# A chunked recurrence and a gated two-product block on one core: both blocks' first products in a row, and weights narrowed in place

## The chip, the cores and the metric

One core of a Trainium2 chip runs the whole program. Its engines work side by side, each through its own queue in order: TensorE (PE in the profile; its weight loads are PEld) multiplies matrices into PSUM, VectorE (DVE), ScalarE (ACT) and GpSimd (POOL) work on elements, and SyncE (SP) issues most transfers. The metric is the device time of the program in microseconds.

## The reference

Two stages. For 4 sequences of 768 tokens and 8 heads of size 64, a state of 64 by 64 per head is decayed and updated at every token, and the query reads it:

```
for t in range(S):
    state = gamma * state + einsum('bhd,bhe->bhde', k[:, :, t], v[:, :, t])
    y[:, :, t] = scale * einsum('bhd,bhde->bhe', q[:, :, t], state)
x = y.transpose(0, 2, 1, 3).reshape(3072, 512)
h = x @ w_in                      # 512 x 2048
out = (h * sigmoid(1.702 * h)) @ w_out   # 2048 x 512
```

q, k and v are float32. The two weights come as 64-bit floats, which the kernel gets as pairs of 32-bit words, and which it has to turn into float32 itself.

## The kernel before

**Chunks and blocks.** The 3072 tokens are 24 chunks of 128, and a block is four chunks (512 tokens). A chunk takes three steps: `turn` (q and k transposed, for blocks 0 and 1 by TensorE, `pt`, for the others by VectorE; GpSimd scales k into `kd`), `attend` (`pa`, q times k for each head, masked by VectorE into `at`) and `finish` (`py`, the output, which VectorE scales into the block's input `X`; `pu`, the update of the state).

**Narrowing.** The weights arrive in 32 pieces of 512 KB, 16 of `w_in` (into tile `W1`) and 16 of `w_out` (into `W2`). `fetch` loads a piece into one of three raw buffers, and `narrow` turns its pairs of words into floats in seven steps, each over 128 partitions by 512 elements: ScalarE takes the high word's magnitude (line 171), GpSimd clamps it (172), VectorE shifts it, joins the sign and cuts out the exponent (173, 174, 175), ScalarE scales the low word (176), GpSimd multiplies it by the exponent (177), and VectorE adds both into the weight tile (180). The raw buffers and two sets of three scratch buffers lie in the part of `W2` that is filled later (slots 4 to 6). The last thing in `narrow` is the next `fetch`, which waits until the raw buffer is free.

**Two forms of a product.** A block's first product (`up`) and second (`down`) exist in a plain form (`up0`, `down0`: 16 steps f of four multiplications of 128 by 128 by 512) and in a form with seven sub-products in place of eight (`up`, `down`), which needs sums of the weights (`sums_w1`, `sums_w2`, on GpSimd), of X (`sums_x`) and of the hidden layer G (`sums_g`). Each step f of the plain first product reads pieces 2p and 2p+1 with p = f // 2, and each step f of the second reads piece 16 + f. Between the products, `hidden` applies the gate: a sigmoid on ScalarE into `sg`, and a multiplication by VectorE (line 253) out of the PSUM tile `ph`. `ph` and the second product's `po` share four PSUM buffers.

**Order of the work.** TensorE's order is the order in which the program is written. The other queues are ordered by the compiler's scheduler. Before, the program runs: the four chunks of block 0 with eight narrowings; block 0's first product, plain, with one narrowing per step; block 0's second product, plain, with the rest of the narrowings, the steps of block 1's four chunks between its steps, and `sums_w1`; then for block 1 and each later one `up` and `down` in the seven-product form, the next block's chunks lying between the units of `down`. `sums_w2` runs beside block 1's `up`.

## Time and profile before

| | us |
|---|---|
| median of 3 runs (lowest, highest) | 781.69 (781.29, 781.89) |
| profiled execution, its own time | 782.11 |
| its span | 780.3 |
| PE busy in the span | 725.1 (93%) |
| DVE busy | 368.6 (47%) |
| POOL busy | 206.3 (26%) |
| ACT busy | 153.4 (20%) |

The profile is of one execution; its time is 0.42 us above the median of the runs. Busy shares are means over stages of different kinds, so they are read stage by stage. A duration includes what an instruction waits after it has started, so the same operation can show two lengths. In the rows, `W` stands for W1 and W2 alike, and the raw and scratch buffers, which lie in W2, have that name too.

### The profile page before, as it was taken

What the parts mean: (1) busy time and instruction counts of PE and PEld (TensorE: products, weight loads), DVE (VectorE), ACT (ScalarE), POOL (GpSimd) and SP (SyncE); (2) the same over time, 40 slices, a digit from 0 to 9 for tenths busy, and PEclk for the clock granted to TensorE, in tenths of its full rate; (3) what the DMA queues carried; (4) which work ended last, traced back from release to release, by engine and by line L of the source; (5) the groups of instructions that cost most, each with busy time, mean ns of one, the idle gap of its engine ahead of it and who ended that gap; (6) DMA issues with size and microseconds to landing.
All of it is one profiled execution on the core that took longest, in us unless ns stands there. A gap on an engine that the chain in (4) does not pass through costs nothing.

```text
span 780.3 us, 9581 instructions
## 1 busy us (share of the span) xinstructions
PE 725.1 (93%) x3648; PEld 572.4 (73%) x3648; DVE 368.6 (47%) x547; ACT 153.4 (20%) x253; POOL 206.3 (26%) x195
## 2 busy tenths in 40 slices
PE   4679677499999999999999999999999999999998
PEld 3454222155568888888888888888888888888886
DVE  3678868761144336334436434445334364244251
ACT  3233334310103310013300023300033200033100
POOL 2776665584140004020014220012300022200030
PEclk9879878699999999999999999999999999999999
DMA  8634323312241003340022331022430030100001
GB/s 202 185 113 149 134 108 109 133 29 55 45 109 23 1 15 77 56 99 14 1 54 53 84 60 22 1 50 55 85 71 1 0 69 13 42 1 1 1 13 41
DMA packets 142253, 46.27 MB, mean 59 GB/s; under 512 B 129920, under 2 KB 135552, under 8 KB 142208
## 3 DMA queue, kind: packets, MB, share of 16 engines
q1 hardware_dynamic: 135504, 39.10, 21.5%
q10 hardware_dynamic: 6704, 6.57, 2.5%
q8 instruction: 29, 0.48, 0.2%
q14 instruction: 16, 0.13, 0.1%
HBM read 39.33 MB, written 6.29 MB: 58 GB/s over the span
## 4 chain that ended last, share of the span: by engine, by line
PE 77%; DVE 11%; POOL 7%; issue 3%; DMA 1%; SPq 0%; ACT 0%; POOLq 0%; DVEq 0%
PE pd L363 30%; PE px L312 18%; PE py L312 13%; PE po L272 5%; PE py L227 4%; POOL W L177 3%; PE pu L237 3%; PE pa L210 3%; DVE W L174 3%; DVE W L180 2%; DVE W L173 2%; PE py L223 2%; DVE W L175 1%; POOL W L172 1%; DMA W<-in_moe_w_in_dram 1%
## 5 line engine op out<-in xcount | busy, mean ns | idle before, releaser
L363 PE MATMUL pd<-W,G 128*128 128x256 f32 x1120 | 250.3, 381 | 0.4 <-DVE G L303 0.3
L363 PEld LDWEIGHTS pd<-W,G 128*128 128x128 f32 x1120 | 210.1, 190 | 30.8 <-DVE G L303 1.2
L312 PE MATMUL px<-X,W 128*128 128x256 f32 x640 | 148.7, 379 | 0.0
L312 PEld LDWEIGHTS px<-X,W 128*128 128x128 f32 x640 | 121.6, 190 | 17.0 <-issue 0.5
L312 PE MATMUL py<-X,W 128*128 128x256 f32 x480 | 113.4, 379 | 0.0
L312 PEld LDWEIGHTS py<-X,W 128*128 128x128 f32 x480 | 91.2, 190 | 12.4
L201 POOL TENSOR_TENSOR kd<-kn_in,cold 128x512 f32<-128x512 f32 x20 | 22.2, 1110 | 294.3 <-PE pu L237 200.4
L260 PE MATMUL ph<-X,W 128*128 128x512 f32 x128 | 65.8, 671 | 16.9 <-DVE G L253 16.9
L272 PE MATMUL po<-W,G 128*128 128x512 f32 x128 | 61.8, 628 | 10.4 <-DVE G L253 10.4
L213 DVE TENSOR_TENSOR at<-pa,mask 128x512 f32<-128x512 f32 x48 | 30.9, 685 | 83.6 <-PE pa L210 83.5
L260 PEld LDWEIGHTS ph<-X,W 128*128 128x128 f32 x128 | 26.6, 214 | 55.4 <-issue 30.9
L304 POOL TENSOR_TENSOR G<-G 128x512 f32<-128x512 f32 x20 | 29.0, 1449 | 111.5 <-DVE G L303 107.0
L272 PEld LDWEIGHTS po<-W,G 128*128 128x128 f32 x128 | 24.3, 199 | 39.2 <-issue 24.9
L252 ACT ACTIVATE sg<-G 128x512 f32<-128x512 f32 x60 | 37.8, 631 | 64.0 <-DVE G L322 38.3
L177 POOL TENSOR_TENSOR W<-W 128x512 f32<-128x512 f32 x32 | 43.5, 1360 | 25.8 <-DVE W L175 25.8
L253 DVE TENSOR_TENSOR G<-G,sg 128x512 f32<-128x512 f32 x60 | 41.3, 689 | 17.4 <-ACT sg L252 17.4
L227 PE MATMUL py<-at,v_in 128*64 128x128 f32 x384 | 32.2, 303 | 11.3 <-DVE at L213 11.3
L180 DVE TENSOR_TENSOR W<-W 128x512 f32<-128x512 f32 x32 | 30.3, 946 | 26.4 <-POOL W L177 26.1
L171 ACT ACTIVATE W<-W 128x512 f32<-128x512 f32 x32 | 21.6, 675 | 87.7 <-DVE W L180 79.1
L227 PEld LDWEIGHTS py<-at,v_in 128*64 128x64 f32 x384 | 24.5, 150 | 17.1 <-DVE at L213 13.7
L210 PEld LDWEIGHTS pa<-qT,kT 64*128 64x128 f32 x384 | 24.1, 193 | 15.4 <-issue 7.3
L322 DVE TENSOR_TENSOR G<-py,p 128x512 f32<-128x512 f32 x20 | 13.8, 692 | 44.4 <-PE py L312 44.4
(66 smaller groups left out, 620.5 us busy)
## 6 DMA issues: line engine op xcount, KB each, us to landing
W<-in_moe_w_in_dram SPq DMA_DIRECT2D x16, 512.0 KB, 4.0
W<-in_moe_w_out_dram SPq DMA_DIRECT2D x16, 512.0 KB, 3.2
v_in<-in_v_dram SPq DMA_DIRECT2D x24, 256.0 KB, 3.3
out_dram<-o ACTq DMA_DIRECT2D x24, 256.0 KB, 2.3
kn_in<-in_k_dram SPq DMA_DIRECT2D x21, 256.0 KB, 3.7
q_sq<-in_q_dram SPq DMA_DIRECT2D x256, 16.0 KB, 1.8
k_sq<-in_k_dram SPq DMA_DIRECT2D x256, 16.0 KB, 1.7
q_in<-in_q_dram SPq DMA_DIRECT2D x8, 256.0 KB, 5.2
```

The source lines that it names most:

```text
L177: pool.tensor_mul(r, r, e)
L180: dve.tensor_add(w, m.rearrange(shape, **sizes), r.rearrange(shape, **sizes))
L210: pe.matmul(p[:, i, hp, :], KT[j][r, hp, :], QT[j][r, hp, :], start=True, stop=True)
L213: dve.tensor_mul(AT[j][:, i], p[:, i], mask[:, i])
L227: pe.matmul(y[i * D:(i + 1) * D, hp, :], vn[:, 2 * hp + i, :], a[:, i, hp, :], start=(not c and hp == 0), stop=(hp == HP - 1), skip_group_ ...
L252: act.activation(s, h, AF.Sigmoid, scale=1.702)
L253: dve.tensor_mul(g, h, s)
L260: pe.matmul(h, w, X[:, c // 2:4:2, c % 2, :], start=(c == 0), stop=(c == 3))
L272: pe.matmul(PO[n], G[:, p, 2 * half + ab, t0:t0 + P], w, start=(f == 0), stop=(f == NFF - 1))
L304: pool.tensor_sub(g[1], g[1], g[0])
L312: pe.matmul(acc[:, u, :], W1[:, 2 * d + u, sa, c, :], X[:, sb, c, :], start=(start and u == 0 and c == 0), stop=(stop and c == 1), skip_gr ...
L363: pe.matmul(p0[:, n, :], G[:, p, sa, n * P:(n + 1) * P], W2[:, sb, p, :], start=(new and p == 0 and n == 0), stop=(last and p == NP - 1), ...
```

## The change

1. **Order.** Block 1's first product now runs in the plain form, right after block 0's first product and ahead of block 0's second. Block 1's chunks, which lay between the steps of block 0's second product, now lie between the steps of block 0's first. Block 1's second product stays in the seven-product form. So `sums_x` is not needed for block 1; `sums_w2` moves to block 0's second product and `sums_w1` to block 1's second. Within block 0, chunk j+1's `turn` is written ahead of chunk j's `finish`, and chunk 4's `turn` comes with block 0.
2. **Places.** Block 1's X lies in slot 6 of W2 (`X1`). Block 0's hidden layer, whose tile G now takes block 1's, lies in slots 4 to 6 of W1, slots 4 to 6 of X and a small tile (`g0`). Since these are not one run, the gate's multiplication of block 0 is two instructions of 256 elements. qT, kT, kd and at of the first eight chunks lie in G, in two sets.
3. **Narrowing in place.** There is no scratch: magnitude and exponent are made in the destination, sign and value in the raw buffer's high words, the scaled low word in its low words. These raw operands have a step of two words. There are four raw buffers. The clamp goes from GpSimd to VectorE.
4. **Loads.** The first eight chunks' q and k are loaded two chunks ahead in `turn`, v in `finish`; block 2's first loads (32 small ones for q and k of a chunk) are written into block 1's first product.

```diff
-    NRAW, NTMP = 3, 2
+    NRAW = 4
...
-            lo, hi = x[:, :, 0], x[:, :, 1]
-            m, e, r = TMPS[i % NTMP]
-            mu, eu = m.bitcast(U32), e.bitcast(U32)
+            (w, _, m), x = PIECES[i], RAWS[i % NRAW]
+            mu = m.bitcast(U32)
+            two_runs = x.rearrange("p (a b) two -> p a b two", a=2)
+            lo, hi = two_runs[:, :, :, 0], two_runs[:, :, :, 1]
 
             act.activation(m, hi.bitcast(F32), AF.Abs, scale=2.0 ** 16)
-            pool.tensor_scalar(m, m, F64_MOST * 2.0 ** 16, F64_LEAST * 2.0 ** 16, op0=ALU.min, op1=ALU.max)
+            dve.tensor_scalar(m, m, F64_MOST * 2.0 ** 16, F64_LEAST * 2.0 ** 16, op0=ALU.min, op1=ALU.max)
             dve.tensor_scalar(mu, mu, 3, None, op0=ALU.logical_shift_left)
-            dve.scalar_tensor_tensor(mu, hi, 0x80000000, mu, op0=ALU.bitwise_and, op1=ALU.bitwise_or)
-            dve.tensor_scalar(eu, mu, 0xFF800000, None, op0=ALU.bitwise_and)
+            dve.scalar_tensor_tensor(hi, hi, 0x80000000, mu, op0=ALU.bitwise_and, op1=ALU.bitwise_or)
+            dve.tensor_scalar(mu, hi, 0xFF800000, None, op0=ALU.bitwise_and)
+            r = lo.bitcast(F32)
             act.activation(r, lo, AF.Copy, scale=2.0 ** -52)
-            pool.tensor_mul(r, r, e)
+            pool.tensor_mul(r, r, m)
...
-        dve.tensor_mul(g, h, s)
+        for g, h, s in [(g, h, s)] if not isinstance(g, list) else [(g[i], h[:, i], s[:, i]) for i in range(2)]:
+            dve.tensor_mul(g, h, s)
...
+    turn(0)
     for j in range(CB):
-        if j + 2 <= CB:
-            load(j + 2)
-        turn(j)
         attend(j)
         narrow(1)
+        turn(j + 1)
         finish(j)
         narrow(1)
+    between = chunks(1)[1:]
     for f in range(NFF):
-        up0(f)
+        up0(0, f)
+        if f < NP or f % 4 == 3:
+            narrow(1)
+        if between and f >= 2:
+            between.pop(0)()
+    for f in range(NFF):
+        up0(1, f)
         narrow(1)
...
+        if f >= NFF - 2:
+            load(2 * CB + f - NFF + 2)
     for f in range(NFF):
         down0(f)
-        narrow(1)
-        if between and f >= 2:
-            between.pop(0)()
         if f % 4 == 3:
-            sums_w1(f // 2 - 1)
-    sums_x()
+            sums_w2(f // 2 - 1)
     for m in range(1, NB):
-        for d in range(NP // 2):
-            up(d)
-            if m == 1:
-                sums_w2(2 * d)
-            if m + 1 < NB and d < 2:
-                load((m + 1) * CB + d)
         between = chunks(m + 1) if m + 1 < NB else []
+        if m > 1:
+            for d in range(NP // 2):
+                up(d)
+                if m + 1 < NB and d < 2:
+                    load((m + 1) * CB + d)
         for n, unit in enumerate(down(m)):
             unit()
+            if m == 1 and n % 8 == 3:
+                sums_w1(n // 4)
```

**TensorE, from block 0's last chunk on, before** (`ph` is the first product, `po` block 0's second, `px` and the `py` of line 312 block 1's first, W_72 is W1 and W_73 is W2):

```order
L223 MATMUL py<-qT,state_81 128x128 x4
L227 MATMUL py<-at,v_in 64x128 x8
L237 MATMUL pu<-v_in,kd 128x128 x4
L260 MATMUL ph<-X,W_72 128x512 x64
L272 MATMUL po<-W_73,G 128x512 x12
L194 MATMUL pt<-ident,q_in 128x128 x4
L194 MATMUL pt<-ident,kn_in 128x128 x4
L272 MATMUL po<-W_73,G 128x512 x4
L210 MATMUL pa<-qT,kT 128x128 x8
```

The same engine now, from block 1's last chunk, between the steps of block 0's first product (`ph<-X`), to block 1's first (`ph<-W_73`, whose input X1 lies in W2) and block 0's second:

```order
L292 MATMUL ph<-X,W_72 128x512 x4
L245 MATMUL py<-G,state_82 128x128 x4
L249 MATMUL py<-G,v_in 64x128 x8
L262 MATMUL pu<-v_in,G 128x128 x4
L292 MATMUL ph<-X,W_72 128x512 x12
L292 MATMUL ph<-W_73,W_72 128x512 x64
L304 MATMUL po<-W_73,W_72 128x512 x6
L304 MATMUL po<-W_73,X 128x512 x2
```

Block 1's 64 multiplications of 512 columns stand ahead of block 0's second product, and nothing of a chunk stands between the steps of the second product any more.

**VectorE, in block 0's first product, before** (173, 174, 175 and 180 are narrowing, 253 is the gate):

```order
L173 TENSOR_SCALAR W_73<-W_73 128x512
L174 SCALAR_TENSOR_TENSOR W_73<-W_73 128x512
L175 TENSOR_SCALAR W_73<-W_73 128x512
L173 TENSOR_SCALAR W_73<-W_73 128x512
L253 TENSOR_TENSOR G<-ph,sg 128x2x256
L180 TENSOR_TENSOR W_72<-W_73 128x2x2x128
```

The same engine now, in block 0's first product (178 is the clamp, 179, 180, 181 and 188 or 191 the other steps of narrowing, 279 the gate, 253 and 267 the end of chunk 6):

```order
L181 TENSOR_SCALAR W_73<-W_73 128x2x256
L279 TENSOR_TENSOR W_72<-ph,sg 128x256
L279 TENSOR_TENSOR X<-ph,sg 128x256
L253 TENSOR_TENSOR W_73<-py,rowd 128x4x128
L267 COPY state_82<-pu 64x4x64 x2
L191 TENSOR_TENSOR W_73<-W_73 128x2x256
L180 SCALAR_TENSOR_TENSOR W_73<-W_73 128x512
L178 TENSOR_SCALAR W_73<-W_73 128x2x256
L181 TENSOR_SCALAR W_73<-W_73 128x2x256
L179 TENSOR_SCALAR W_73<-W_73 128x2x256
```

The clamp has joined VectorE's queue, the gate is two rows, and the chunks' rows lie among the narrowings. The last narrowing addition stands behind the gate of step 1 of block 1's first product:

```order
L279 TENSOR_TENSOR G<-ph,sg 128x2x256
L181 TENSOR_SCALAR W_73<-W_73 128x2x256
L179 TENSOR_SCALAR W_73<-W_73 128x2x256
L180 SCALAR_TENSOR_TENSOR W_73<-W_73 128x512
L191 TENSOR_TENSOR W_73<-W_73 128x2x256
L181 TENSOR_SCALAR W_73<-W_73 128x2x256
L279 TENSOR_TENSOR G<-ph,sg 128x2x256
L191 TENSOR_TENSOR W_73<-W_73 128x2x256
L279 TENSOR_TENSOR G<-ph,sg 128x2x256 x14
```

All but two of the gates of block 1's first product stand behind all narrowing.

More of the change, by code (lines that the diff above doesn't have):

```diff
@@ L111, in load @@
         if j < 2 * CB:
-            plain("q", q, "q_sq", 2)
-            plain("kn", k, "k_sq", 2)
+            if "q" in what:
+                plain("q", q, "q_sq", 2)
+                plain("kn", k, "k_sq", 2)
         else:
@@ L124, in load @@
                 plain("kn", k, "kn", 1)
-        plain("v", v, "v", 2)
+        if "v" in what:
+            plain("v", v, "v", 2)
     w1v = moe_w_in.bitcast(U32).rearrange("(c p) (f two) -> p c f two", p=P, two=2)
     w2v = moe_w_out.bitcast(U32).rearrange("(f p) (e two) -> p f e two", p=P, two=2)
-    stage = W2[:, 4:7].rearrange("p s n e -> p (s n e)")
-    NRAW, NTMP = 3, 2
-    RAWS = [stage[:, 1024 * i:1024 * (i + 1)].bitcast(U32).rearrange("p (n two) -> p n two", two=2)
-            for i in range(NRAW)]
-    TMPS = [[stage[:, 1024 * NRAW + 512 * (3 * i + t):1024 * NRAW + 512 * (3 * i + t + 1)] for t in range(3)]
-            for i in range(NTMP)]
+    NRAW = 4
+    RAWS = [W2[:, 4 + i // 2, i % 2 * 4:i % 2 * 4 + 4].rearrange("p n e -> p (n e)").bitcast(U32)
+            .rearrange("p (n two) -> p n two", two=2) for i in range(NRAW)]
     PIECES = []
@@ L404 @@
     load(1)
-    fetch()
-    fetch()
+    for _ in range(NRAW - 1):
+        fetch()
     make_identity(nc, ident)
@@ L418 @@
         dve.memset(t, 0.0)
-    for j in range(CB):
-        if j + 2 <= CB:
-            load(j + 2)
-        turn(j)
-        attend(j)
-        narrow(1)
-        finish(j)
-        narrow(1)
-    for f in range(NFF):
-        up0(f)
-        narrow(1)
-    narrow(1)
     def chunks(m):
```

67 lines of the change are left out of this document (48 added, 19 removed).

## The prediction

> **What bounds the kernel now.** I read first the windows of the trace, cut where the work changes: block 0's attention up to the first gate (62.7 us), the stage up to the last narrowing addition (171.2), block 0's second product and block 1's first (to 276.3), and the rest.
>
> ```profile
> core 0: us, PE busy (x) PEld busy (x) DVE busy (x) ACT busy (x) POOL busy (x), PEclk, DMA share, GB/s
> 10.00:62.70 52.70, 37.46 (x225) 28.24 (x226) 35.16 (x55) 16.94 (x29) 32.84 (x33) 0.87 0.58 158
> 62.70:171.20 108.50, 81.25 (x175) 33.29 (x174) 81.84 (x110) 36.99 (x63) 72.08 (x65) 0.84 0.34 114
> 171.20:276.30 105.10, 104.41 (x501) 74.09 (x500) 36.83 (x56) 19.86 (x34) 24.36 (x22) 1.00 0.21 43
> 276.30:780.30 504.00, 499.81 (x2744) 435.30 (x2742) 212.60 (x319) 77.96 (x128) 74.15 (x68) 1.00 0.18 38
> ```
>
> From 171.2 on TensorE is busy 104.41 of 105.10 us and then 499.81 of 504.00: nothing but its own work counts there. Before that no engine is full. In the second row VectorE has 81.84 and GpSimd 72.08 of 108.50, so I looked at how these two stand to each other, in the instructions in order of time, VectorE's first and then GpSimd's in the same stretch.
>
> ```profile
> 109.41 1.09 DVE L180 TENSOR_TENSOR W<-W 128x512 f32<-128x512 f32 x1 [0.85 <-POOL W L177]
> 110.42 0.41 DVE L173 TENSOR_SCALAR W<-W 128x512 uint32<-128x512 uint32 x1
> 110.87 0.69 DVE L174 SCALAR_TENSOR_TENSOR W<-W 128x512 uint32<-128x512 uint32 x1
> 111.59 0.72 DVE L175 TENSOR_SCALAR W<-W 128x512 uint32<-128x512 uint32 x1
> 112.23 0.41 DVE L173 TENSOR_SCALAR W<-W 128x512 uint32<-128x512 uint32 x1
> 112.68 1.63 DVE L174 SCALAR_TENSOR_TENSOR W<-W 128x512 uint32<-128x512 uint32 x1
> 114.24 0.68 DVE L253 TENSOR_TENSOR G<-ph,sg 128x512 f32<-128x512 f32 x1
> 114.84 0.68 DVE L180 TENSOR_TENSOR W<-W 128x512 f32<-128x512 f32 x1
> ```
>
> ```profile
> 108.11 1.27 POOL L177 TENSOR_TENSOR W<-W 128x512 f32<-128x512 f32 x1 [1.21 <-DVE W L175]
> 109.34 0.61 POOL L172 TENSOR_SCALAR W<-W 128x512 f32<-128x512 f32 x1
> 111.29 0.75 POOL L172 TENSOR_SCALAR W<-W 128x512 f32<-128x512 f32 x1 [1.33 <-ACT W L171]
> 112.40 1.37 POOL L177 TENSOR_TENSOR W<-W 128x512 f32<-128x512 f32 x1 [0.36 <-DVE W L175]
> ```
>
> Line 174 takes 0.69 us at 110.87, but 1.63 at 112.68, where GpSimd's multiplication had begun at 112.40: that ends at 113.77, and 174 ends 0.54 later. Line 180 at 109.41 is stretched to 1.09 by the clamp of 109.34. So VectorE's narrowing steps, which read and write SBUF, and GpSimd's operations take turns: their lengths alone add up. The gate (253), which reads PSUM, is not stretched; the groups of the stage below show it at a mean of 680 ns, and likewise the chunks' steps 213, 230 and 246. [...]
>
> ```profile
> L253 DVE TENSOR_TENSOR G<-ph,sg 128x512 f32<-128x512 f32 x16 | 10.9, 680 | 0.2 <-ACT sg L252 0.2
> L213 DVE TENSOR_TENSOR at<-pa,mask 128x512 f32<-128x512 f32 x8 | 5.1, 686 | 0.1
> L230 DVE TENSOR_TENSOR X<-py,rowd 128x512 f32<-128x512 f32 x4 | 2.8, 689 | 4.2 <-PE py L227 4.2
> L246 DVE TENSOR_TENSOR state<-state,pu 64x256 f32<-64x256 f32 x6 | 2.5, 419 | 2.4 <-PE pu L237 2.3
> ...
> L177 POOL TENSOR_TENSOR W<-W 128x512 f32<-128x512 f32 x32 | 43.5, 1360 | 25.8 <-DVE W L175 25.8
> ...
> L244 POOL TENSOR_TENSOR state<-state,cold 64x256 f32<-64x256 f32 x8 | 6.2, 778 | 0.3
> L284 POOL TENSOR_TENSOR W<-W 128x512 f32<-128x512 f32 x4 | 6.0, 1493 | 0.0
> ...
> L201 POOL TENSOR_TENSOR kd<-kn_in,cold 128x512 f32<-128x512 f32 x4 | 4.2, 1044 | 7.9 <-issue 4.3 <-PE pu L237 3.6
> ...
> L289 POOL TENSOR_TENSOR W<-W 128x512 f32<-128x512 f32 x1 | 1.3, 1258 | 0.0
> ```
>
> **The sum of before, 10 to 171.2 us,** in lengths alone. VectorE: 32 pieces of 0.41 + 0.69 + 0.41 + 0.69 = 70.4; 16 gates of 0.68, 10.9; four chunks with 8 masks (5.5), 4 outputs (2.8) and 8 state steps of 0.42 (3.4): 93.0. GpSimd: 32 clamps of 0.61, 19.5; 32 multiplications of 1.27, 40.6; 22 weight sums (lines 281 to 290) of 1.26, 27.7; kd 4.2; state 6.2: 98.2. Together 191.2, in 161.2 us: 0.843 of the sum, 30 us being saved where PSUM-fed VectorE work runs beside GpSimd and where ends and starts overlap. The narrowing stage is that sum, and TensorE waits for it.
>
> **The change, part by part.** *Narrowing.* The clamp leaves GpSimd (0.61) and costs VectorE what the shift costs, 0.41, the nearest row. Multiplication, joins and addition stay; per piece 2.61 us of VectorE and 1.27 of GpSimd. The steps on raw words have a step of two now. Line 174 already reads such words and takes the 0.69 of line 180, whose operands are in a row: lower bound no cost, which I take. The upper bound is half speed for the stepped multiplication, 1.27 more per piece, and 0.69 for the exponent cut, 0.28 more.
>
> *Weight sums.* All 16 sums of W1 leave the stage, and 4 sums of W2 (5.0) are left in it. The others come behind the last narrowing, under 55 us of block 0's second product and then block 1's second; 28 of them are 35 us of GpSimd. W1's sums are needed only at block 2. Without that cover, 35 us.
>
> *Gates and chunks.* Block 0's gates become 32 of 256 elements, at the 0.42 of line 246's size 13.4; two whole ones of block 1 come in front of the last addition (1.4). Eight chunks instead of four lie in the stage: 16 masks 11.0, 8 outputs 5.5, 14 state steps 5.9; on GpSimd 8 kd 8.3 and 12 state steps of 0.78, 9.4. Two transpositions for block 2 at an output's 0.69, 1.4.
>
> Sum: VectorE 32 x 2.61 + 13.4 + 1.4 + 11.0 + 5.5 + 5.9 + 1.4 = 122.1; GpSimd 40.6 + 8.3 + 9.4 + 5.0 = 63.3; together 185.4. At the same 0.843, 156.3 us: the last addition begins at **166.3**, 4.9 us earlier. The factor's bounds: the 14.7 us by which PSUM-fed work grows (22.6 to 37.2) may all lie under GpSimd, 12.4 earlier; or the 30 us saved shrink with GpSimd's share to 19.3, 9.8 later.
>
> *TensorE behind it.* The chain that ended last has TensorE's lengths when it doesn't wait.
>
> ```profile
> 171.18 1.74 DVE W L180
> ...
> 208.94 0.87 PE pt L194 x8
> ...
> 213.25 1.09 PE pa L210 x16
> ...
> 217.97 0.89 PE py L223 x8
> 218.87 1.02 PE py L227 x16
> 219.89 1.09 PE pu L237 x8
> 220.98 6.87 PE po L272 x16
> 227.85 1.73 PE px L312 x8
> ...
> 276.19 6.91 PE pd L363 x32
> ```
>
> Two plain steps are 6.87 us, 3.44 each; a seven-product first product is 276.19 - 227.85 = 48.3. Block 1's, in plain form, is 16 x 3.44 = 55.0, so TensorE has 6.7 us **more** to do. But it does it earlier. Before, 105.0 us lie between the last addition (171.18) and block 1's second product (276.19). Now, four PSUM buffers let TensorE be through step 4 when step 1's gate frees the next one, just ahead of the last addition: 11 steps are left (37.8), then block 0's second product (55.0), 92.8 us. Block 1's second product begins at 166.3 + 92.8 = 259.1, **17.1 us** earlier. Behind it the program is as it was, with 35 us of weight sums spread under it. The profiled execution's 782.11 becomes 765.0; the median is 0.42 lower, 764.6.
>
> *Chunk order and loads.* `turn` ahead of `finish` gives TensorE something to do while VectorE masks; I count nothing for it, since the sum above, not TensorE, sets the stage. Block 2's loads now lie in SP's queue between the fetches of `w_out`. Sixteen small ones took:
>
> ```profile
> 228.09 10.88 SPq L120 DMA_DIRECT2D q_sq<-in_q_dram  x16
> ```
>
> that is 0.68 us each, up to six between two fetches, 4.1 us. A fetch is let go when the piece four earlier is added, so it has three pieces of 156.3 / 32 = 4.9 us, 14.7, in hand: covered. Without that, up to 32 x 0.68 = 22 us.
>
> **The rivals.**
> 1. *TensorE sets the pace.* If narrowing hides better, the floor is TensorE's own work. Up to the first gate the sum falls from 61.5 (narrowing 18.7, chunks 11.7, GpSimd 31.1) to 54.9 (21.6, 11.7, 21.6), so at the first stage's 52.7 / 61.5 that gate comes at about 57. Then 16 steps (55.0) with chunk 4's rest, 5, 6 and 7 (17.0 from the chain's rows) are 72 us at full clock or 86 at the granted 0.84, and 32 steps more 110.0: block 1's second product then begins at 239 to 253, a gain of 23 to 37. For it: the PSUM-fed work. Against: the order puts most gates right behind an addition, when GpSimd has just finished. Time 755 (745 to 759).
> 2. *Serial coupling.* VectorE's queue now holds rows that wait for TensorE (chunks, gates) among the narrowings, and half the 30 us saved are lost: 170.4 in place of 156.3, a gain of 3, about 779. For it: each wait on TensorE holds the narrowing behind it. Against: TensorE has slack in that stage. If nothing at all were saved, 794.
> 3. *Stepped operands are slow* (the other side). The place is GpSimd's multiplication, which reads and writes every second word, and the exponent cut on VectorE, which reads so. It decides from 17.1 / (32 x 0.843) = 0.63 us per piece on. [...] For it: no row shows GpSimd on such operands. Against: line 174. [...]
> 4. *No change in effect*: the plain form's 6.7 us and the longer VectorE queue just cancel the earlier start; it is the end of rival 2 and has no chance of its own.
>
> **How the numbers follow.** Forecast 0.52 (765, its own range 752 to 774 from the factor's bounds), rival 1 0.18, rival 2 0.16, rival 3 0.14. A difference of 0.2% (1.6 us) is about what can be told from no change here. Faster: the first two and two thirds of rival 2, 0.80; within 0.2%: 0.05; slower: rival 3 and the end of rival 2, 0.15. The range takes in rival 1 and the cheaper part of rival 3: 749 to 787.
>
> **What would show it.** The last narrowing addition near 166 us, and TensorE without gaps from there; 92.8 us later the first `pd`. Line 184 at 1.27 us alone and line 181 at 0.41 say that stepped operands cost nothing. Both engines together still fill the stage, with GpSimd's share down by a third. Wrong would be: TensorE waiting in block 0's second product, additions later than 185 us, fetches that arrive after VectorE asks, or a first product in which TensorE never waits.

## The result, and the profile after

The changed kernel takes **759.47 us** (median of 4 runs, 757.97 to 760.20) against 781.79 for the kernel before on the same chip: a ratio of **0.9712** with a 95% interval of 0.9695 to 0.9729. The forecast was 765.0 us, with a range of 749 to 787.

The profiled execution's page gives TensorE this share of a span of 757.6 us (before: 780.3). Below it the windows of the trace after, cut where the work changes: up to 52.0 block 0's chunks, up to 161.6 the stage that ends with the last narrowing addition, up to 253.5 the rest of block 1's first product and block 0's second, then block 1's second product and all that follows.

```profile
PE 722.7 (95%) x3552; PEld 553.2 (73%) x3552; DVE 358.5 (47%) x579; ACT 145.2 (19%) x241; POOL 179.0 (24%) x159
```

```profile
core 0: us, PE busy (x) PEld busy (x) DVE busy (x) ACT busy (x) POOL busy (x), PEclk, DMA share, GB/s
10.00:52.00 42.00, 30.57 (x221) 24.55 (x222) 33.25 (x55) 17.25 (x29) 18.11 (x17) 0.88 0.79 191
52.00:161.60 109.60, 98.56 (x369) 51.48 (x368) 97.57 (x179) 42.07 (x72) 48.73 (x39) 0.94 0.53 141
161.60:253.50 91.90, 91.45 (x214) 40.32 (x213) 12.52 (x17) 7.17 (x12) 33.56 (x27) 1.00 0.05 10
253.50:757.60 504.10, 499.95 (x2745) 435.42 (x2743) 212.98 (x319) 77.44 (x127) 75.73 (x70) 1.00 0.19 39
```

The last window is what it was (504.10 against 504.00 us). The whole gain lies ahead of it: block 1's second product begins at 253.4 in place of 276.0. In the second window TensorE is now busy 98.56 of 109.60, VectorE 97.57 where the corresponding stage before had 81.84 of 108.50, and GpSimd 48.73 where it had 72.08. In the third window TensorE is busy 91.45 of 91.90.

The chain that ended last (start and length in us), from the last narrowing addition (191) over the gate (279) to block 1's second product:

```profile
161.61 1.74 DVE W L191
163.35 0.61 DVE G L279
...
164.00 34.60 PE ph L292 x80
198.60 54.93 PE po L304 x128
253.54 6.91 PE pd L395 x32
```

From 164.0 on TensorE has 80 matmuls of block 1's first product left, ten steps, then 128 of block 0's second. That is the shape the prediction gave it, with one step less.

What TensorE waited for between 44 and 175 us, before and after (total us, times, longest):

```profile
PE ph L260 <- DVE G L253: 16.9, 8, 4.3
PE po L272 <- DVE G L253: 10.4, 3, 5.2
PE py L227 <- DVE at L213: 3.6, 4, 2.7
```

```profile
PE py L249 <- DVE G L235: 9.5, 8, 3.1
PE ph L292 <- DVE G L279: 2.5, 3, 1.2
PE ph L292 <- DVE X L253: 1.7, 1, 1.7
```

Before, it waited for gates (253). Now it waits for the masks of block 1's chunks (235), and less. So two things are candidates for what sets the time of the changed kernel, and the experiments are built to tell them apart:

- **Theory A, the prediction's:** the lengths of VectorE's narrowing steps and of GpSimd's work add up, their sum sets when the last addition comes, and a fixed rest of TensorE work follows.
- **Theory B, its first rival's:** TensorE's own path sets the time: when its first `ph` starts, its own work, and what it waits for on the way. The narrowings matter only as far as masks and gates stand behind them in VectorE's queue.

TensorE's path can be balanced from its records: from the first `ph` to the first `pd` lies TensorE's own work, its waits, and half of the time in which it worked while its granted clock was half (before, eight `ph` that began at 81.93 took 5.40 us with 3.4 us at a granted 0.50 among them, and the eight at 88.89, at 1.00, 3.70). Before: 55.6 to 276.0 us, with 27.9 us of waits and 34.1 us at half clock, of which 10.2 lie inside waits and 23.9 are work. After: 50.1 to 253.4, with 11.5 us of waits and 13.7 at half clock, 0.7 inside a wait and 13.0 work. The 22.6 us are thus an earlier start (5.5), fewer waits (16.4) and less work at half clock (10.9 / 2 = 5.5), less 4.8 of added work (220.4 - 27.9 - 12.0 = 180.5 before, 203.3 - 11.5 - 6.5 = 185.3 after). The plain form adds 6.7; 0.9 goes because chunk 4's `turn` now lies ahead of the first `ph` (0.87 us in the chain before); 1.0 isn't traced.

### The profile page after: what moved, and what is told of

Its sections match the earlier page's. It is cut to its first block, busy times and chain, and to the rows that moved or that the text cites. A ratio compares the mean times of both kernels' runs of the same rounds, so it can differ in the third digit from the quotient of the medians.

```text
span 757.6 us, 9340 instructions
## 1 busy us (share of the span) xinstructions
PE 722.7 (95%) x3552; PEld 553.2 (73%) x3552; DVE 358.5 (47%) x579; ACT 145.2 (19%) x241; POOL 179.0 (24%) x159
## 4 chain that ended last, share of the span: by engine, by line
PE 76%; DVE 3%; POOL 1%; DMA 0%; issue 0%; ACT 0%; DVEq 0%; POOLq 0%; ACTq 0%
PE pd L395 31%; PE px L344 15%; PE py L344 11%; PE po L304 7%; PE ph L292 5%; PE pa L232 2%; PE py L249 2%; PE pu L262 2%; PE py L245 2%; DVE G L334 1%; DVE G L335 0%; DMA W<-in_moe_w_out_dram 0%; DVE W L180 0%; POOL W L184 0%; DVE G L333 0%; DVE W L191 0%
## 5 line engine op out<-in xcount | busy, mean ns | idle before, releaser
L344 PE MATMUL px<-X,W 128*128 128x256 f32 x512 | 119.0, 379 | 0.0
L344 PEld LDWEIGHTS px<-X,W 128*128 128x128 f32 x512 | 97.3, 190 | 13.2
L344 PE MATMUL py<-X,W 128*128 128x256 f32 x384 | 90.7, 379 | 0.0
L344 PEld LDWEIGHTS py<-X,W 128*128 128x128 f32 x384 | 73.0, 190 | 9.9
L292 PE MATMUL ph<-W,W 128*128 128x512 f32 x128 | 55.9, 595 | 2.5 <-DVE G L279 2.5
L292 PEld LDWEIGHTS ph<-W,W 128*128 128x128 f32 x128 | 24.1, 190 | 34.2 <-issue 28.9
L304 PE MATMUL po<-W,W 128*128 128x512 f32 x96 | 42.5, 592 | 0.0
L277 ACT ACTIVATE sg<-G 128x512 f32<-128x512 f32 x48 | 30.3, 631 | 50.9 <-DVE G L354 30.6
L279 DVE TENSOR_TENSOR G<-G,sg 128x512 f32<-128x512 f32 x48 | 33.1, 689 | 13.7 <-ACT sg L277 13.7
L277 ACT ACTIVATE sg<-ph 128x512 f32<-128x512 f32 x32 | 18.9, 594 | 60.6 <-PE ph L292 42.7
L184 POOL TENSOR_TENSOR W<-W 128x512 f32<-128x512 f32 x16 | 23.2, 1452 | 29.0 <-DVE W L181 15.7
L184 POOL TENSOR_TENSOR W<-W,W 128x512 f32<-128x512 f32 x16 | 22.0, 1375 | 30.7 <-DVE W L181 13.7
## 6 DMA issues: line engine op xcount, KB each, us to landing
W<-in_moe_w_in_dram SPq DMA_DIRECT2D x16, 512.0 KB, 3.8
W<-in_moe_w_out_dram SPq DMA_DIRECT2D x16, 512.0 KB, 3.4
```

Of the source, the lines that this page charges most:

```text
L184: pool.tensor_mul(r, r, m)
L277: act.activation(s, h, AF.Sigmoid, scale=1.702)
L279: dve.tensor_mul(g, h, s)
L292: pe.matmul(h, w, x[:, c // 2:4:2, c % 2, :], start=(c == 0), stop=(c == 3))
L304: pe.matmul(PO[n], g0(p, 2 * half + ab)[:, t0:t0 + P], w, start=(f == 0), stop=(f == NFF - 1))
L344: pe.matmul(acc[:, u, :], W1[:, 2 * d + u, sa, c, :], X[:, sb, c, :], start=(start and u == 0 and c == 0), stop=(stop and c == 1), skip_gr ...
```

## The experiments

For each kernel of this study, read from its trace: first `ph`, the last narrowing addition, the end of TensorE's last wait ahead of `pd` with the `ph` matmuls that TensorE then still had to do, its waits from the first `ph` on, and the first `pd`. The ratio is to the kernel before. Times of the trace are those of one execution, the last column is the median of several; for order_only and pool_order the traced execution was 2.3 and 2.5 us below that median. The recorded expectations call theory A the turn-taking theory; theory B appears there as rival 1 and as the lockstep theory.

| kernel | first `ph` | last addition | last wait ends, `ph` left | waits | first `pd` | median us, ratio (95%) |
|---|---|---|---|---|---|---|
| before | 55.6 | 171.2 | - | 27.9 | 276.0 | 781.8 |
| the change | 50.1 | 161.6 | 164.0, 80 | 11.5 | 253.4 | 759.47, 0.9712 (0.9695 to 0.9729) |
| inplace_old_order | 58.2 | 167.3 | - | 28.1 | 273.6 | 780.31, 0.9981 (0.9972 to 0.9990) |
| order_only | 47.1 | 164.9 | 167.3, 88 | 21.1 | 261.8 | 770.18, 0.9855 (0.9840 to 0.9870) |
| clamp_pool | 50.9 | 161.0 | 163.5, 104 | 18.5 | 263.2 | 769.11, 0.9839 (0.9823 to 0.9854) |
| no_clamp | 47.6 | 147.3 | 148.8, 104 | 12.6 | 250.2 | 756.07, 0.9669 (0.9653 to 0.9685) |
| turn_undone | 57.4 | 164.7 | 166.0, 96 | 12.6 | 262.3 | 768.84, 0.9838 (0.9824 to 0.9851) |
| sp_order | 51.1 | 164.5 | 165.8, 88 | 17.3 | 260.3 | 766.35, 0.9803 (0.9785 to 0.9821) |
| pool_order | 49.3 | 163.3 | 165.7, 72 | 13.1 | 251.6 | 760.14, 0.9716 (0.9696 to 0.9735) |
| mask_gap | 51.9 | 164.2 | 161.8, 88 | 14.3 | 255.0 | 759.80, 0.9721 (0.9707 to 0.9736) |
| paced | 49.1 | 189.2 | 68.5, 224 | 3.2 | 237.1 | 751.35, 0.9609 (0.9594 to 0.9624) |
| mul_vector | 45.6 | 149.5 | none | 0.0 | 229.6 | 735.97, 0.9408 (0.9394 to 0.9421) |
| mul_both | 46.4 | 168.6 | 170.4, 48 | 9.1 | 246.0 | 751.99, 0.9621 (0.9607 to 0.9634) |
| add_only | 34.6 | 89.0 | none | 0.0 | 217.4 | 723.93, 0.9263 (0.9251 to 0.9276) |

An edit changes more than the lines shown, because the compiler's scheduler orders VectorE's queue anew for each kernel. If clamp and multiplication are left aside, VectorE's order departs from that of the changed kernel within the first 23 of some 230 instructions (up to 260 us) in clamp_pool, no_clamp, turn_undone and mul_vector, at the 52nd in pool_order, the 87th in mask_gap and the 120th in sp_order. Differences between these kernels therefore hold the edit and a new order together, and no run here takes the two apart. mul_vector and mul_both have one and the same order on VectorE.

### The two halves of the change apart

**Narrowing in place, in the old order of blocks.** Into the kernel before went the new narrowing alone (four raw buffers, clamp on VectorE).

```
 # the kernel before, with
-            pool.tensor_scalar(m, m, F64_MOST * 2.0 ** 16, F64_LEAST * 2.0 ** 16, op0=ALU.min, op1=ALU.max)
+            dve.tensor_scalar(m, m, F64_MOST * 2.0 ** 16, F64_LEAST * 2.0 ** 16, op0=ALU.min, op1=ALU.max)
...
-            dve.scalar_tensor_tensor(mu, hi, 0x80000000, mu, op0=ALU.bitwise_and, op1=ALU.bitwise_or)
+            dve.scalar_tensor_tensor(hi, hi, 0x80000000, mu, op0=ALU.bitwise_and, op1=ALU.bitwise_or)
...
-            pool.tensor_mul(r, r, e)
+            pool.tensor_mul(r, r, m)
```

> The kernel before with the new narrowing alone (in place, four raw buffers, clamp on VectorE), its order of the work kept. By the prediction's sum: VectorE 32 x 2.61 + 10.9 + 11.7 = 106.1, GpSimd 98.2 - 19.5 = 78.7, together 184.8 in place of 191.2, the last addition 5.4 us earlier, about 776.4. If stepped operands or the longer VectorE queue eat that: 782 or more. If the changed kernel's whole gain lies in the narrowing: 760.

It gives 780.31 us: 0.2% faster, where the sum expected 776.4. The last addition comes 3.9 us earlier (5.4 by the sum), but the first `ph` starts 2.6 us later and TensorE's waits stay (28.1).

**The order of blocks, with the old narrowing.** Into the changed kernel went the old narrowing (three raw buffers, scratch for the three temporaries, clamp on GpSimd); block 1's input has a place of its own.

```
-    X1 = W2[:, 6].rearrange("p (s c) t -> p s c t", s=4)
+    X1 = const.tile([P, 4, 2, TH], F32, name="X1")
...
-    NRAW = 4
...
+    NRAW, NTMP = 3, 2
...
-            dve.tensor_scalar(m, m, F64_MOST * 2.0 ** 16, F64_LEAST * 2.0 ** 16, op0=ALU.min, op1=ALU.max)
+            pool.tensor_scalar(m, m, F64_MOST * 2.0 ** 16, F64_LEAST * 2.0 ** 16, op0=ALU.min, op1=ALU.max)
...
-            pool.tensor_mul(r, r, m)
+            pool.tensor_mul(r, r, e)
```

> The new order and places with the old narrowing (scratch buffers in slots 4 to 6 of W2, three raw buffers, clamp on GpSimd); block 1's X, and later qT, kT and at, in a tile of their own. By the turn-taking sum alone: 6.4 us more of GpSimd and VectorE than the change, about 765. Lockstep theory (TensorE, whose chunks wait for masks in VectorE's queue, sets the pace together with it): no better than the clamp on GpSimd alone, 769 or more, and with two scratch sets in place of four raw buffers rather 770 to 776. If the gain needs the narrowing in place: 780.

770.18 us, within what the lockstep theory expected; the sum alone gave 765. The order alone gives 11.3 us (0.0145 x 782), the narrowing alone 1.5 (0.0019 x 782), both together 22.3: the halves need each other. With the old narrowing TensorE waits 21.1 us in the new order, with the new one 11.5.

### Does the last addition set the end?

**The clamp back on GpSimd**, and **no clamp at all** (weights beyond its range are then not held).

```
-            dve.tensor_scalar(m, m, F64_MOST * 2.0 ** 16, F64_LEAST * 2.0 ** 16, op0=ALU.min, op1=ALU.max)
+            pool.tensor_scalar(m, m, F64_MOST * 2.0 ** 16, F64_LEAST * 2.0 ** 16, op0=ALU.min, op1=ALU.max)
```

> The changed kernel with the clamp back on GpSimd, all else as changed. Turn-taking theory (VectorE's SBUF steps and GpSimd's operations add up; the changed kernel's stage of 151.6 us is 0.818 of its sum of 185.4): the sum grows by 32 x (0.61 - 0.41) = 6.4 us, the stage by 5.2, about 764.7 us. Rival 1 (TensorE sets the pace of the stage): 759.5, no change. Rival V (VectorE's own queue sets it, GpSimd runs freely beside): VectorE loses 32 x 0.41 = 13.1 us, about 749.

```
-            dve.tensor_scalar(m, m, F64_MOST * 2.0 ** 16, F64_LEAST * 2.0 ** 16, op0=ALU.min, op1=ALU.max)
```

> The changed kernel with the clamp left out altogether (weights out of the clamp's range would not be held to it). Turn-taking theory: the sum falls by 32 x 0.41 = 13.1 us, the stage by 10.7, about 749. Rival 1 (TensorE sets the pace): TensorE is busy 98.6 of the second stage's 109.6 us, so next to nothing is gained, 757 to 759.5. Rival V (VectorE alone): 13.1 less, 746.5.

With the clamp on GpSimd the last addition comes 0.6 us **earlier** than in the changed kernel, and the time is 9.6 us **longer**. Without a clamp it comes 14.3 us earlier, and the time falls by only 3.4. By theory A alone neither can be: it expected 764.7 and 749. None of the three expectations held for clamp_pool (769.11); no_clamp (756.07) came 1 us below the range of rival 1. The chains of clamp_pool and of no_clamp show where the time went:

```profile
163.51 44.87 PE ph L292 x104
208.39 54.93 PE po L304 x128
263.32 6.91 PE pd L395 x32
```

```profile
140.09 0.43 SPq L125
140.56 1.48 DMA q_sq<-in_q_dram
...
147.35 0.69 DVE W L190
...
148.85 46.57 PE ph L291 x104
195.42 54.93 PE po L303 x128
250.35 5.83 PE pd L394 x27
```

TensorE's last wait ends at 163.5 in clamp_pool, 0.5 us earlier than the 164.0 of the changed kernel, but 104 `ph` matmuls are left behind it, not 80: 44.87 against 34.60 us, the 10 us by which `pd` is late. In no_clamp the wait ends 15.2 us earlier, and 12.0 of these are eaten behind it: 10.4 by the same backlog of 24 more matmuls, the other 1.6 by the clock, which is granted at 0.72 on average from 148.85 to 155.0. So the rest behind the last addition is not fixed: it is what TensorE couldn't do ahead, and that depends on its waits earlier on (18.5 us in clamp_pool). Why clamp_pool waits longer isn't shown: the clamp's place and VectorE's order changed together. The end of the last wait, plus 0.43 us for each `ph` left, plus 54.9 us gives the first `pd` of all the kernels in the table that still wait near the end, to within 0.3 us; only order_only, no_clamp and sp_order come 1.5 us later: their 88, 104 and 88 `ph` took 39.73, 46.57 and 39.73 us, 0.45 each. This is bookkeeping, since TensorE doesn't stop behind its last wait; it says where the time is, not why the wait ended then.

In no_clamp rows of another kind stand on the chain: block 2's loads (125) in SP's queue, up to 140.5. That doesn't make these loads late. The trace puts none of VectorE's idle time between 60 and 200 us down to a load, and the transposition of block 2's keys (218), which reads the last of them, follows the instruction ahead of it without a gap. Such rows stand on the chains of turn_undone, sp_order and mask_gap as well, and not on that of the changed kernel. The prediction had these loads covered, and no run here speaks against it.

### The pieces of the order

**`turn` behind, as it was.**

```
-    turn(0)
     for j in range(CB):
+        turn(j)
         attend(j)
         narrow(1)
-        turn(j + 1)
         finish(j)
         narrow(1)
-    between = chunks(1)[1:]
+    between = chunks(1)
```

> The changed kernel with block 0's chunks in the old order of steps (turn, attend, narrowing, finish, narrowing; chunk 4's turn between the steps of the first product). The prediction counted nothing for this edit: 759.5. Lockstep theory: the first product's start, 55.6 us before and 50.1 after the change, moves back by up to 5.5 us and the end with it, 762 to 765.

768.84 us, 9.4 longer than the change and more than either expectation (759.5, 762 to 765). The first `ph` starts at 57.4 in place of 50.1, the waits hardly change (12.6), and 96 matmuls, 41.47 us, are left behind the last one.

The prediction counted this part of the change as nothing; without it, two fifths of the gain are lost. The edit undoes two things, chunk j+1's `turn` ahead of chunk j's `finish` and chunk 4's `turn` ahead of the first product, and VectorE's order is another one; what each of the three costs wasn't tried apart.

**SP's queue in program order**, so that block 2's loads come behind the fetches, and **GpSimd's in program order**, so that the sums of W2 come behind the multiplications.

```
-    ctx.enter_context(tc.manual_schedule(engines={mybir.EngineType.PE}))
+    ctx.enter_context(tc.manual_schedule(engines={mybir.EngineType.PE, mybir.EngineType.SP}))
```

> The changed kernel with SyncE's queue in the order in which the program is written: all fetches of weights ahead of block 2's small loads, which come behind the last fetch. The prediction's term (loads between the fetches are covered by three pieces in hand): no change, 759.5. Rival (ScalarE's 32.1 us of waits for pieces of w_out hold the narrowing; the chain that ended last holds some 9 us of that transfer): 5 to 9 us less, 751 to 755. If the loads then come too late for block 2's first chunk, TensorE waits in block 1's second product and part of it is given back.

```
-    ctx.enter_context(tc.manual_schedule(engines={mybir.EngineType.PE}))
+    ctx.enter_context(tc.manual_schedule(engines={mybir.EngineType.PE, mybir.EngineType.Pool}))
```

> The changed kernel with GpSimd's queue in the order in which the program is written, so that all sums of W2 come behind the last narrowing multiplication. Turn-taking theory: 4 sums of 1.26 leave the stage, 5.0 x 0.818 = 4.1 us less, about 755.4; if they stand where nothing else covers, the whole stretching of VectorE's last steps (some 7 us) goes, 752. Rival 1 (TensorE sets the pace): no change, 759.5.

sp_order: 766.35 us, 6.9 longer, where 759.5 or 751 to 755 was expected. Taking the loads away from between the fetches gains nothing. The transposition of block 2's first keys on VectorE (219) moves from 141.7 to 167.5, and TensorE's waits grow from 11.5 to 17.3; that the later load is the cause isn't shown, and in mul_both the same transposition starts at 168.0 with 9.1 us of waits. pool_order: 760.14 us, no difference to the change, as rival 1 expected (theory A: 755.4). Moving W2's sums behind the multiplications, and all of GpSimd's work into program order with them, gains nothing.

**A step of room behind each mask.** Block 1's chunks were rearranged so that another chunk's transpositions stand between a mask and the output that reads it.

```
-    between = chunks(1)[1:]
+    between = [lambda: attend(CB)]
+    for j in range(CB, 2 * CB):
+        between.append((lambda j=j: turn(j + 1)) if j + 1 < 2 * CB else (lambda: None))
+        between.append(lambda j=j: finish(j))
+        if j + 1 < 2 * CB:
+            between.append(lambda j=j: attend(j + 1))
```

> The changed kernel with block 1's chunk steps in another order between the steps of block 0's first product: the next chunk's turn stands between a chunk's attend and its finish (and one empty step ahead of the last finish), so that two steps of the product in place of one lie between the attention scores and the output that needs their mask. VectorE and GpSimd do the same work. Turn-taking theory (their sum sets the stage): 759.5. Lockstep theory: TensorE's 9.5 us of waits for masks, and some of the 6.8 us that it loses to the halved clock behind them, go away, 747 to 753.

759.80 us, no difference, as theory A expected; the lockstep theory had expected 747 to 753. Its waits of TensorE, total us, times, longest:

```profile
PE py L249 <- DVE G L235: 5.1, 2, 4.4
PE py L245 <- ACT G L217: 4.4, 2, 4.1
```

The waits for masks fall from 9.5 to 5.1 us, and two for the transposed queries, 4.4 us in all, take their place. This rearrangement of TensorE's order only moved the wait.

### Whose queue is it?

**VectorE and GpSimd in an order made by hand.** A piece's addition is written one step behind its other steps, a gate one step behind its product, and 24 pieces in place of 26 are narrowed beside the first products, the rest under block 0's second.

```
-    ctx.enter_context(tc.manual_schedule(engines={mybir.EngineType.PE}))
+    ctx.enter_context(tc.manual_schedule(engines={mybir.EngineType.PE, mybir.EngineType.DVE, mybir.EngineType.Pool}))
...
-        up0(0, f)
-        if f < NP or f % 4 == 3:
-            narrow(1)
+        gates.append(up0(0, f))
+        if f:
+            gates.pop(0)()
+        second()
+        if f % 4 != 3:
+            first()
...
-        up0(1, f)
-        narrow(1)
+        gates.append(up0(1, f))
+        gates.pop(0)()
+        second()
+        if f % 3 != 2:
+            first()
```

> VectorE and GpSimd also work through their instructions in the order in which the program writes them, and that order is made by hand: a piece's addition is written one step behind its other steps, a gate one step behind its first product, and fewer pieces are narrowed beside the first products (24 in place of 26), the rest under block 0's second product. If TensorE waits because its masks, outputs and gates stand behind narrowings in a queue that the scheduler filled, its waits between the first first product and block 1's second product fall from 11.5 us to about 5, and block 1's second product begins near 245 in place of 253.4: about 751 us. If the sum of the narrowing steps sets the stage, the last addition stays near 161.6 and the time near 759.5. Against both: in program order VectorE also stalls in the steady stages, where the scheduler had found something to do; each stalled output of a second product of 7 us then shows, and the time is 762 to 775.

751.35 us, as theory B expected, 8.1 less than the change, although the last addition comes 27.6 us **later** (189.2). TensorE's waits from the first `ph` on fall to 3.2 us, and the chain has all of block 1's first product, with the last 24 matmuls of block 0's, in one piece:

```profile
117.09 65.24 PE ph L298 x152
182.33 54.93 PE po L319 x128
237.26 6.91 PE pd L410 x32
```

It begins block 1's second product 16.3 us earlier and gives half of it back later: the window of the second product and what follows is 512.0 us long in place of 504.1, and one wait there is 4.9 us for block 2's keys, transposed late in VectorE's program order.

```profile
PE pa L238 <- DVE kT L225: 4.9, 1, 4.9
```

**The multiplication on VectorE.**

```
-            pool.tensor_mul(r, r, m)
+            dve.tensor_mul(r, r, m)
```

> The multiplication by the low words' scale goes from GpSimd (1.29 us) to VectorE, whose additions of the same size take 0.69. The sum of the two engines' lengths falls by 32 x 0.58 = 18.6 us, while VectorE's own queue grows by 32 x 0.69 = 22.1. If that sum sets the stage, the last addition comes 0.843 x 18.6 = 15.7 us earlier than 161.6, near 146, and the time near 744. If TensorE's own path sets it, by way of its masks and gates in VectorE's queue, block 1's second product stays within 4 us of 253.4, and the time is 756 to 764.

**735.97 us**, 23.5 less than the change and some 46 less than before: the best kernel of the study that does all the work. Its stage and what follows up to the first `pd`:

```profile
49.50:149.50 100.00, 100.00 (x393) 51.24 (x392) 99.17 (x206) 44.58 (x76) 14.99 (x13) 1.00 0.58 156
149.50:229.60 80.10, 80.10 (x188) 35.39 (x187) 9.29 (x14) 4.79 (x8) 31.20 (x26) 1.00 0.05 10
```

TensorE is busy 100.00 of 100.00 us: it waits for nothing. Neither expectation holds. Theory B's 756 to 764 took it that VectorE, with 22 us more in its queue, would hold TensorE longer. Theory A's sum gave a last addition 15.7 us earlier, where 12.1 were measured, and a time of 744; the kernel is 8 us faster than that. TensorE's 11.5 us of waits are gone, and its first `ph` starts 4.5 us earlier. Since it never waits, its own path sets the end here, as theory B has it, and the last addition doesn't: 80.1 us lie between that and the first `pd`, where the change has 91.8. What VectorE got for the 22 us shows in its groups (busy us, mean ns, idle before them and releaser; 10 to 185 us), in the change and then with the multiplication on VectorE:

```profile
L178 DVE TENSOR_SCALAR W<-W 128x512 f32<-128x512 f32 x32 | 23.4, 737 | 5.8 <-ACT W L177 5.7
...
L188 DVE TENSOR_TENSOR W<-W 128x512 f32<-128x512 f32 x16 | 14.5, 912 | 10.4 <-POOL W L184 10.4
...
L191 DVE TENSOR_TENSOR W<-W 128x512 f32<-128x512 f32 x16 | 12.1, 754 | 5.3 <-POOL W L184 5.3
```

```profile
L178 DVE TENSOR_SCALAR W<-W 128x512 f32<-128x512 f32 x32 | 15.6, 494 | 7.4 <-ACT W L177 7.4
...
L188 DVE TENSOR_TENSOR W<-W 128x512 f32<-128x512 f32 x16 | 12.3, 770 | 0.0
L191 DVE TENSOR_TENSOR W<-W 128x512 f32<-128x512 f32 x16 | 11.5, 719 | 0.0
```

Two things go at once: the additions' waits for GpSimd's product (10.4 + 5.3 = 15.7 us), and the turns with GpSimd that stretch the steps (the clamp alone from 737 to 494 ns, 7.8 us over 32).

**The multiplication on VectorE, and a square on GpSimd that nobody needs.** To tell those two apart, GpSimd squares the same words behind each multiplication, into a tile of its own. VectorE's order is the same, and nothing on VectorE waits for the square.

```
+    idle = const.tile([P, 512], mybir.dt.bfloat16, name="idle")
...
             dve.tensor_mul(r, r, m)
+            pool.tensor_mul(idle, r, r)
```

> The multiplication is on VectorE, and for each piece GpSimd then squares the same low words into a tile that nobody reads (128x512 at a step of two, as before its multiplication was: 1.29 us). VectorE's instructions stand in the same order as with the multiplication on VectorE alone, and none of them waits for GpSimd's square; only the next fetch into the piece's buffer does, and it has three pieces in hand. It tells two things apart that went away together: VectorE's turns with GpSimd, and its waits for GpSimd's product. If the turns are what the narrowing costs, the last addition comes at 149.5 + 0.843 x 32 x 1.29 = 184 at most, or some 25 us later than 149.5 if the lengths overlap as the ends did; TensorE waits again, block 1's second product begins 10 to 30 us later than 229.6, and the time is 746 to 766. If the waits for GpSimd's product and the in-order queue behind them were the cost, the last addition stays within 4 us of 149.5, TensorE doesn't wait, and the time is 735 to 738.

751.99 us: 16.0 longer. VectorE has no wait for GpSimd, but its additions have become long. From the first `ph` to the last addition it is busy all but 0.9 us:

```profile
46.40:168.60 122.20, 113.76 (x408) 57.59 (x407) 121.34 (x214) 44.33 (x76) 47.94 (x40) 0.96 0.48 132
```

ScalarE waits longer for its pieces than in mul_vector (56.4 us in place of 39.5 between 10 and 170), but with VectorE as full as that, later pieces aren't what holds it.

A stretch in order of time, VectorE's steps and then GpSimd's:

```profile
134.25 0.68 DVE L185 TENSOR_TENSOR W<-W 128x512 f32<-128x512 f32 x1
134.85 0.42 DVE L180 TENSOR_SCALAR W<-W 128x512 uint32<-128x512 uint32 x1
135.18 1.52 DVE L193 TENSOR_TENSOR W<-W 128x512 f32<-128x512 f32 x1
136.63 0.68 DVE L181 SCALAR_TENSOR_TENSOR W<-W 128x512 uint32<-128x512 uint32 x1
137.23 0.41 DVE L281 TENSOR_TENSOR W<-ph,sg 128x256 f32<-128x256 f32 x1
```

```profile
135.06 1.10 POOL L186 TENSOR_TENSOR idle<-W 128x512 bf16<-128x512 f32 x1 [3.22 <-DVE W L185]
```

The square runs from 135.06 to 136.16; the addition (193) that begins at 135.18 ends at 136.70, 1.52 us in place of 0.68, without depending on it. Over all pieces:

```profile
L193 DVE TENSOR_TENSOR W<-W 128x512 f32<-128x512 f32 x16 | 22.1, 1383 | 0.0
L190 DVE TENSOR_TENSOR W<-W 128x512 f32<-128x512 f32 x16 | 19.7, 1232 | 0.0
```

Against 719 and 770 ns that is (22.1 - 11.5) + (19.7 - 12.3) = 18.0 us, and the last addition comes 19.1 us later. So the turns alone, with a GpSimd instruction of 1.10 us per piece, cost 16 us of the whole kernel. They don't add the whole length: 32 squares are 35.2 us, and 19.1 of these came onto the last addition, less than the 25 expected. The other 7.5 us between the change and mul_vector are net: the waits for the product go, a longer GpSimd instruction goes, 32 multiplications come to VectorE.

### The floor

**Fetch and addition alone.** All other steps of the narrowing are left out, so the weights are not the reference's.

```
-            act.activation(m, hi.bitcast(F32), AF.Abs, scale=2.0 ** 16)
...
-            pool.tensor_mul(r, r, m)
...
-                dve.tensor_add(w, xf[:, :, :, :, 1], xf[:, :, :, :, 0])
+                dve.tensor_add(w, xf[:, :, :, :, 1], xf[:, :, :, :, 1])
```

> Only the fetch and the addition of each piece are left (the addition reads the high words twice); scaling, clamp, shift, join, exponent cut and multiplication are left out, so the weights are not the reference's. Per piece 0.69 us remains of 3.88. It measures the floor of TensorE's path in this order of work. If waits on masks come from narrowings ahead of them in VectorE's queue, they go with the narrowings: from the first first product to block 1's second product 184 to 188 us in place of 203.3, the first first product begins near 45, and block 1's second product near 232: about 738 us. If they come from the order of the chunks itself, 8 us or more of waits stay, and the time is 744 to 752.

723.93 us, 14 less than expected: from the first `ph` to the first `pd` it is 182.8 us without a wait, just under the 184 to 188 expected, but the first `ph` starts at 34.6, not near 45, since VectorE is free for block 0's chunks too. The waits for masks do go with the narrowings, so the order of the chunks itself costs none. mul_vector, with 184.0 us from `ph` to `pd`, has only its later start left: 45.6 - 34.6 = 11.0 of the 12.0 us between the two.

## Why the prediction came out, point by point

*VectorE and GpSimd take turns.* Right, and now measured by itself: mul_both. That "their lengths alone add up" is too strong: there about half of GpSimd's length was added (19.1 of 35.2 us).

*The sum, 185.4 us at a factor of 0.843, last addition at 166.3.* It came at 161.6: 151.6 us from 10 on, a factor of 0.818. The bounds given (12.4 earlier, 9.8 later) hold it. As a rule to a few us the sum fails: clamp_pool's is 6.4 us longer than the change's, and its last addition comes 0.6 earlier.

*Stepped operands cost nothing.* Right. The groups of the multiplication (184) and of the exponent cut (181), min/median/max ns:

```profile
L184 POOL TENSOR_TENSOR W<-W,W x16: 1287/1325/1619, 13.6 to 92.7; 128x512 f32<-128x512 f32 x16
L181 DVE TENSOR_SCALAR W<-W x32: 411/419/1111, 12.3 to 158.8; 128x512 uint32<-128x512 uint32 x32
```

1.287 us undisturbed against 1.258 for operands in a row, and 0.411 for the cut; rival 3 needed 0.63 us more per piece. The range's upper end, 787, stands for (787 - 765) / (32 x 0.843) = 0.82 us per piece; no run shows such a term: the multiplication took 0.03 more and the cut nothing.

*TensorE behind it: 11 steps and 55.0, 92.8 us.* Measured 91.8, with ten steps left. That these are so close is partly luck: one step less is 3.2 us, and 2.4 us from the start of the addition, over the gate, to TensorE's first matmul had no term. 259.1 - 253.4 = 5.7 us by which block 1's second product came before the forecast: 4.7 from the sum, 1.0 from here. **But this step holds only for this kernel.** It was put as work that is always left behind the last addition. The table shows 48 to 104 matmuls left, by what TensorE waited for earlier; clamp_pool and no_clamp, which leave that step untouched, move the end by 9.8 later and 3.2 earlier where the last addition moves 0.6 and 14.3 earlier.

*"The sum above, not TensorE, sets the stage", and with it `turn` ahead of `finish` at nothing.* **The step that failed.** turn_undone is 9.4 us slower. In the changed kernel both limits are on: the last addition stands on the chain, and how far TensorE has come by then decides what is left behind it. Rival 1, TensorE's own pace, so had a share in it; but TensorE still waits 11.5 us, 253.4 lies at the late end of its 239 to 253, and 759.47 just above its 745 to 759. Its floor was too high: mul_vector gets to 229.6, because the first `ph` can start earlier than was allowed for.

*Weight sums out of the stage.* Taking out the four left there, counted at 5.0 us, gained nothing (pool_order). What removing the other 18 from the stage is worth by itself wasn't tried.

*Loads of block 2 between fetches: covered, with three pieces in hand.* No load of block 2 is on the chain of the changed kernel. In no_clamp, turn_undone, sp_order and mask_gap some are, and VectorE has no idle time for them there. The fetches themselves are not as well covered as was said. One stands on the chain, and ScalarE, which begins a piece, waits for them (10 to 170 us):

```profile
141.19 3.34 DMA W<-in_moe_w_out_dram
```

```profile
ACT W L177 <- DMA W<-in_moe_w_out_dram: 32.1, 13, 4.9
```

What that costs wasn't tried by itself; mul_vector, whose TensorE waits for nothing, has the same four buffers.

*What would show it: GpSimd's share down by a third, TensorE without gaps from the last addition on.* Both came: 48.73 us in place of 72.08 in the stage, and 91.45 of 91.90 busy behind it.

*Rival 2, serial coupling.* The waits are there (15.7 us of VectorE for GpSimd's product), but the sum came out shorter than forecast, not longer.

*What had no term:* the half clock. Its 5.5 us belong to the gain on TensorE's path, and the windows of before had shown it (0.87 and 0.84 in the column PEclk); only rival 1 reckoned with it. The forecast came out without it since it counted from the last addition on, where the granted clock is 1.00 in both kernels.

## What to carry to other kernels

An operation that is moved from VectorE to GpSimd hadn't left VectorE here, where both work on SBUF: it cost part of its length in VectorE's neighbours (19.1 of 35.2 us in mul_both), and the wait for its result (15.7 us in the change). 32 multiplications of 0.69 us on VectorE cost less than 32 of 1.29 on GpSimd (735.97 against 759.47 us).

When a stage feeds an engine, the end is the last wait's end plus what that engine couldn't do ahead. Count both: a change that ends the feeding earlier gains little if the engine has fallen behind by then, and one that ends it 27.6 us later can gain 8.

Where a scheduler orders the queues, an edit of one line is also a new order. The pair that told most here, mul_vector and mul_both, is the one in which VectorE's order stayed.

## What the runs showed of the hardware

TensorE's granted clock fell to half after some waits of about 2 us (1.88 in mul_both; 2.09 in the change, up to 89.10, with 0.50 from 90.45 on), and not after others (1.74 in the change, up to 50.11; 2.68 in clamp_pool). In mul_both it waited 1.88 us for a mask (first row; idle time and releaser in brackets), and the trace, cut every 3.4 us from 97.40 on, reads:

```profile
99.23 0.43 PE L251 MATMUL py<-G,v_in 128*64 128x128 f32 x2 [1.88 <-DVE G L237]
```

```profile
97.40:100.80 3.40, 1.40 (x16) 1.04 (x16) 3.40 (x8) 1.71 (x3) 0.51 (x1) 1.00 0.49 119
100.80:104.20 3.40, 3.40 (x12) 2.55 (x11) 3.40 (x7) 1.25 (x2) 1.10 (x1) 0.50 0.35 94
104.20:107.60 3.40, 3.40 (x14) 1.79 (x13) 3.34 (x7) 1.23 (x3) 1.41 (x3) 1.00 0.63 178
```

After the window in which TensorE was busy 1.40 of 3.40 us, the next one is granted 0.50, although it is busy throughout. Such a stretch of 3.4 us at half clock costs TensorE 1.7 us: before, the eight `ph` at 81.93 with one among them took 5.40 us, the eight at 88.89 without one 3.70. In the change the clock was at 0.50 for 3.4 us from 70.0 and from 90.45 on.

The length of the wait alone doesn't settle it. In clamp_pool TensorE's last wait, 2.68 us up to 163.51, is followed by full clock:

```profile
160.00:163.50 3.50, 0.83 (x2) 0.02 (x2) 2.53 (x4) 0.02 (x1) 3.50 (x3) 1.00 0.21 33
163.50:170.30 6.80, 6.79 (x16) 3.13 (x17) 2.45 (x4) 1.76 (x3) 2.79 (x3) 1.00 0.35 67
```

What else it takes, no run here shows.
